# A weight product in plain float32 instead of three split products, and five converted layer-1 units ahead instead of two

## The chip, the cores and the metric

The kernel runs on one core of one Trainium2 chip. The metric is device time in microseconds (us) of one execution. Five engines work side by side, each through its own instructions in order: PE (TensorE, matrix products; its weight loads are listed as PEld), DVE (VectorE), ACT (ScalarE), POOL (GpSimd) and SP (SyncE, which here only issues transfers).

## The reference

Attention with normalised queries and keys, then two feed-forward blocks, in float32:

```python
q_n, k_n = rmsnorm(q, g_q), rmsnorm(k, g_k)        # 4 x 12 heads, 448 x 64
attn = softmax(q_n @ k_n.T / 8); x = attn @ v       # x: 1792 x 768
a = x @ w1; b = x @ w2                              # 768 x 1024 each
h = a * b @ w3                                      # 1024 x 1024
x = h @ w_out                                       # 1024 x 768
h = x @ w_in                                        # 768 x 2048
out = (h * clip(h + 3, 0, 6) / 6) @ w_out2          # 2048 x 768
```

The weights arrive as float64, the rest as float32.

## The kernel before

The 48 heads are taken as 24 pairs. Attention of a pair is eight steps; in step s PE makes two score products (L566, L567), DVE scales them and takes the row maximum (L573, L580), ACT the exponential (L585); eight steps later PE transposes (L592, four 112x112 pieces), ACT and DVE split the result into a high and a low part (L601, L611), and PE multiplies by v (L644, L645; for the first two pairs, which stay in plain float32, L640 and L626).

Around the attention steps `fill` feeds PE with other products. First comes `wprime`: (a*b) @ w3 @ w_out is computed as (a*b) @ (w3 @ w_out), and `wprime` makes w3 @ w_out once, as 128 products of a 128x128 piece of w3 with a 128x384 piece of w_out. It is written to memory in `evac` (ACT L223, DVE L224). Then follow `layer1` and `layer2` for the four batches of 448 tokens (L340, L345, and `mm3`, L81 to L83). When attention is over, PE goes on with layers 1 and 2 and then with the second feed-forward block.

Most products are made from split operands: a float32 value is kept as two rounded parts (float32r tiles), and `mm3` adds three products of parts. A weight unit on its way to such a pair costs: a load of float64 into one of four `raw` buffers, `convert` to float32 (ACT L137, L138, then DVE L140, L143), a copy of the high part (ACT L203) and a subtraction for the low part (POOL L205). These items form the list `order` in `open_wprime`: 16 halves of w3 ("a", 512 columns), 16 halves of w_out ("c", 384 columns), and 4 halves of w1 and w2 ("l") that give the first two units of layer 1. The other 14 units of layer 1 are converted in `open_l1` (ACT L287, POOL L289) while layer 1 runs. `rate` says how many us of PE work and of conversion work `fill` adds per attention step. A scheduler then fixes the order of instructions on each engine at build time.

In this text an attention step's number is the count of score pairs (L566 with L567) that stand before it on PE, or of L573 on DVE.

Of the kernel before, what the change touches and what calls it, by code (L numbers as in the profile page):

```python
# [12 lines left out]
F32 = mybir.dt.float32  # L13
F32R = mybir.dt.float32r
I32 = mybir.dt.int32
# [11 lines left out]
P = 128  # L27
# [3 lines left out]
DM = H * D  # L31
KD = DM // P
F1 = 1024
M1 = F1 // P
F2 = 2048
M2 = F2 // P
NH = DM // 2
# [3 lines left out]
LG = 8  # L41
AHEAD = 3
K3 = 12
SHIFT = {'ssum': -1, 'vsplit': -2, 'load_v': 2, 'rsum1': -1, 'ksplit': 4, 'rms1': 0}


@with_exitstack
def fused_kernel(ctx: ExitStack, tc: tile.TileContext, nat, qT, kT, vin, gq, gk,
                 w12, w3t, wo, win, wo2, outT):
    nc = tc.nc  # L50
# [5 lines left out]
    w12d = dpool.tile([M1, 2, P, 2 * DM], F32, name="w12d")  # L56
# [23 lines left out]
    def mm3(ps, lh, ll, rh, rl, first, last):  # L80
        nc.tensor.matmul(ps, lh, rh, start=first, stop=False)  # L81
        nc.tensor.matmul(ps, lh, rl, start=False, stop=False)  # L82
        return nc.tensor.matmul(ps, ll, rh, start=False, stop=last)  # L83
# [4 lines left out]
    def dma(out, src):  # L88
        return nc.sync.dma_start(out, src)
# [67 lines left out]
    W = {}  # L157

    def open_wprime():
        W["head"] = tc.tile_pool(name="head", bufs=1, side="right")  # L160
        W["hp"] = W["head"].__enter__()
        W["cm"] = tc.tile_pool(name="wprime", bufs=1, side="right")
        pool = W["cm"].__enter__()
        woh, w3, raw = {}, {}, {}
        HF = F1 // 2
        halves = [(a, h) for a in range(2, M1) for h in range(2)]
        order = [("a", 0, 0), ("a", 1, 0)] + [("c", c, 0) for c in range(4)] + [("a", 0, 1), ("a", 1, 1)]
        order += [("c", c, 0) for c in range(4, M1)] + [("c", c, 1) for c in range(M1)]
        order += [("a", a, h) for a, h in halves]
        order += [("l", z, h) for z in (1, 0) for h in range(2)]  # L170
        W["first"] = {}
        place = {o: q for q, o in enumerate(order)}
        W.update(pool=pool, woh=woh, w3=w3, place=place, free=0)

        def load(q):
            if q < len(order):
                kind, n, z = order[q]
                if kind == "a":
                    src = w3t[n][:, z * HF : z * HF + HF]
                else:  # L180
                    src = (wo[n] if kind == "c" else w12[0, n])[:, z * NH : z * NH + NH]
                raw[q] = fetch(pool, src, src.shape[1], "raw", 4)

        def item(q):
            kind, n, z = order[q]
            r = raw.pop(q)
            w = r.shape[1]
            if kind == "c":
                t = pool.tile([P, 2, NH], F32R, tag="woh", bufs=2 * M1, name="woh")
                woh[n, z] = (t[:, 0, :], t[:, 1, :])  # L190
            elif kind == "l":
                if z == 0:
                    W["first"][n] = W["hp"].tile([P, 2, DM], F32R, tag="ws", bufs=2, name="ws")
                t = W["first"][n][:, :, z * NH : z * NH + NH]
            else:
                t = pool.tile([P, 2, HF], F32R, tag="w3", bufs=4, name="w3")
                w3[n, z] = (t[:, 0, :], t[:, 1, :])
            f = r
            if r.dtype != F32:
                wi = r[:, :, 0]  # L200
                yield from convert(wi, r)
                f = wi.bitcast(F32)
            nc.scalar.activation(t[:, 0, :], f, AF.Copy)  # L203
            yield w / 1200
            W["sub"] = nc.gpsimd.tensor_sub(t[:, 1, :], f, t[:, 0, :])  # L205
            if kind == "l" and z == 1:
                dma(w12d[0, n], W["first"][n].bitcast(F32).rearrange("p t c -> p (t c)"))
            load(q + 4)
            yield 0.0

        for q in range(4):
            load(q)
        prep[0] = Prep([partial(item, q) for q in range(len(order))],
                       lambda: place["c", M1 - 1, 1] + (W["free"] if W["free"] < len(halves) else 99))

    def wprime():
        pool, place = W["pool"], W["place"]

        def evac(a, n, ps):
            h = NH // P  # L220
            st = pool.tile([P, h, 2, P], F32R, tag="wst", bufs=2, name="wst")
            src = ps[:, :NH].rearrange("p (n c) -> p n c", c=P)
            nc.scalar.activation(st[:, :, 0, :], src, AF.Copy)  # L223
            nc.vector.tensor_sub(st[:, :, 1, :], src, st[:, :, 0, :])  # L224
            for i in range(h):
                j, c = divmod((n * h + i) * M1 + a, 6)
                dma(wpd[j, :, c], st[:, i].bitcast(F32).rearrange("p t c -> p (t c)"))

        def mul(a, n, c, ps):
            h, l = W["w3"][a, c // 4]  # L230
            cs = slice(c % 4 * P, c % 4 * P + P)
            wh, wl = W["woh"][c, n]
            mm3(ps[:, :NH], h[:, cs], l[:, cs], wh, wl, c == 0, c == M1 - 1)

        def ready(a, n, c):
            return prep[0].ready(place["a", a, c // 4]) and prep[0].ready(place["c", c, n])

        for group in [(0, 1)] + [(a,) for a in range(2, M1)]:
            for n in range(2):
                acc = [bank("f") for _ in group]  # L240
                for c in range(M1):
                    for a, ps in zip(group, acc):
                        while not ready(a, n, c):
                            yield None
                        mul(a, n, c, ps)
                        yield 3 * 0.163
                    if n == 1 and c % 4 == 3:
                        W["free"] += len(group)
                for a, ps in zip(group, acc):
                    later(evac, a, n, ps)  # L250
        yield None
        yield None
        W["cm"].__exit__(None, None, None)
        open_l1()

    L = {}
# [3 lines left out]
    def open_l1():  # L260
        L["cm"] = tc.tile_pool(name="l1", bufs=1, side="right", **RW)
        pool = L["cm"].__enter__()
        raw, ws = defaultdict(list), {}
        L.update(ws=ws, xhl={}, abh={}, cur=0, pool=pool)
        pieces = [(u, h) for u in range(2, 2 * M1) for h in range(2)]
        pieces.reverse()

        def load():
            if pieces:
                u, h = pieces.pop()  # L270
                raw[u].append(fetch(pool, w12[u // 2, 1 - u % 2][:, h * NH : h * NH + NH], NH, "raw", 4))

        def item(u):

            if u < 2:
                ws[u] = W["first"][1 - u]
                return
            r = u % NU
            t = (W["hp"] if u % 5 < 2 else pool).tile([P, 2, DM], F32R, tag="ws", bufs=2 if u % 5 < 2 else 3, name="ws")
            if u < 2 * M1:  # L280
                for h, f in enumerate(raw.pop(u)):
                    cs = slice(h * NH, h * NH + NH)
                    if f.dtype != F32:
                        w = f[:, :, 0]
                        yield from convert(w, f)
                        f = w.bitcast(F32)
                    nc.scalar.activation(t[:, 0, cs], f, AF.Copy)  # L287
                    yield 0.35
                    nc.gpsimd.tensor_sub(t[:, 1, cs], f, t[:, 0, cs])  # L289
                    load()  # L290
                    yield 0.0
                dma(w12d[r // 2, 1 - r % 2], t.bitcast(F32).rearrange("p t c -> p (t c)"))
            else:
                src = w12d[r // 2, 1 - r % 2] if r < 2 * M1 else wpd[r - 2 * M1].rearrange("p k c -> p (k c)")
                dma(t.bitcast(F32).rearrange("p t c -> p (t c)"), src)
                yield 0.0
            ws[u] = t

        for _ in range(4):
            load()  # L300
        prep[0] = Prep([partial(item, u) for u in range(B * NU)], lambda: L["cur"] + AHEAD)
        for _ in range(4):
            prep[0].step()

    def xsplit(i):
# [106 lines left out]
    def attention(ap, rate):  # L412
# [185 lines left out]
        def thi(i, kb):  # L598
            ps, hi, lo = T["X", i, kb]
            if kb != 3 or i < K3 or full(i):  # L600
                nc.scalar.activation(hi, ps, AF.Copy)  # L601
# [188 lines left out]

    def rate(t):
        if "pool" not in L:
            return 1.05, 2
        if L["cur"] < 8:
            return 2.5, 4
        return 1.6, 2
# [6 lines left out]
    order = [B - 1] + list(range(B - 1))  # L803
# [53 lines left out]
    step, q = 0, 0  # L857
# [35 lines left out]
    for b, t in enumerate(order):  # L893
        acc = None
        for m in range(M2):
# [18 lines left out]
            ps = bank("s", "h2")  # L914
# [14 lines left out]
            u = lp.tile([P, S], F32, tag="u", bufs=2, name="u")  # L929
# [61 lines left out]
```

## Time and profile before

| | us |
|---|---|
| median of 3 runs | 1224.61 |
| the runs | 1225.72, 1224.61, 1220.15 |
| span of the profiled execution | 1219.5 |
| PE, DVE, ACT, POOL busy | 1160.4, 756.6, 726.6, 464.9 |

The profiled execution is known by its span alone; the runs are 0.7 to 6.2 us longer than it. "Busy" of PE is counted from modelled ends of pipelined products, so that a busy PE may still have room; the distance from one product's start to the next is the better measure.

### The profile page before, as it was taken

The numbers are of one execution on the slowest core, as the hardware profiler recorded it, in microseconds if no ns is written. First come the engines' busy times: TensorE is split into PE (matmuls) and PEld (weight loads), VectorE is DVE, ScalarE is ACT, GpSimd is POOL, SyncE is SP. The second block draws the span as 40 slices with busy tenths as digits, with TensorE's granted clock in tenths as the row PEclk, the third lists the DMA queues.
The fourth block names the chain that finished last, engine by engine and source line by source line (L and its number), as shares of the span: only waits on it lengthen the run. The fifth ranks groups of instructions, "written<-read, shape, count | busy, mean of one in ns | idle before, by whom it ended". The sixth has DMA issues, their size and how long they took to land.

```text
span 1219.5 us, 16961 instructions
## 1 busy us (share of the span) xinstructions
PE 1160.4 (95%) x5868; PEld 1020.5 (84%) x5868; DVE 756.6 (62%) x1474; ACT 726.6 (60%) x1401; POOL 464.9 (38%) x316
## 2 busy tenths in 40 slices
PE   3699998899999999999999999999999999999998
PEld 2457887777788999899999998999999999999997
DVE  6977888899976787677633447884333433343332
ACT  6888788899866767666634436664433443344332
POOL 3534224645522213212020005555455445544452
PEclk9799998999999999999999999999999999999999
DMA  7668565788987677666459985430200020001001
GB/s 277 209 220 239 191 188 196 251 284 293 334 265 254 222 224 249 228 240 197 148 187 360 355 304 207 156 101 23 91 1 1 4 88 1 1 1 46 1 1 46
DMA packets 64694, 203.73 MB, mean 167 GB/s; under 512 B 8544, under 2 KB 25440, under 8 KB 64608
## 3 DMA queue, kind: packets, MB, share of 16 engines
q1 hardware_dynamic: 64608, 202.65, 49.4%
q8 instruction: 46, 0.75, 0.3%
q14 instruction: 40, 0.33, 0.1%
HBM read 173.93 MB, written 28.68 MB: 166 GB/s over the span
## 4 chain that ended last, share of the span: by engine, by line
PE 75%; DVE 7%; ACT 5%; DMA 5%; issue 4%; POOL 3%; SPq 0%; ACTq 0%; POOLq 0%; DVEq 0%
PE bank L340 10%; PE acc L81 7%; PE acc L83 7%; PE acc L82 6%; PE h L81 6%; PE h L82 6%; PE h L83 6%; PE bank L345 5%; PE bank L592 4%; PE bank L81 3%; PE bank L82 3%; PE bank L83 3%; DVE PP L573 2%; PE bank L566 2%; PE bank L567 2%
## 5 line engine op out<-in xcount | busy, mean ns | idle before, releaser
L852 POOL TENSOR_TENSOR wis<-wf,wis 128x768 fp32r<-128x768 f32 x63 | 120.0, 1904 | 220.0 <-ACT wis L851 219.9
L340 PE MATMUL bank<-xhl,ws 128*128 128x448 f32 x768 | 184.9, 372 | 2.5 <-ACT bs L316 2.4
L931 DVE SCALAR_TENSOR_TENSOR u<-u,h 128x448 f32<-128x448 f32 x64 | 39.5, 618 | 210.6 <-ACT u L930 210.6
L340 PEld LDWEIGHTS bank<-xhl,ws 128*128 128x128 f32 x768 | 145.1, 191 | 16.5 <-ACT bs L316 3.1
L852 POOL TENSOR_TENSOR wos<-wf,wos 128x768 fp32r<-128x768 f32 x64 | 121.4, 1896 | 91.0 <-ACT wos L851 91.0
L585 ACT ACTIVATE PP<-PP,mx 112x448 f32<-112x448 f32 x192 | 127.2, 664 | 45.0 <-DVE mx L580 36.4
L573 DVE CUSTOM_DVE_ANT_0 PP<-bank,rb,rq 112x448 f32<-112x448 f32 x192 | 129.0, 675 | 34.8 <-PE bank L567 23.9
L83 PE MATMUL acc<-g,wos 128*128 128x448 f32 x384 | 141.3, 368 | 0.0
L82 PE MATMUL acc<-g,wos 128*128 128x448 f32 x384 | 141.3, 368 | 0.0
L81 PE MATMUL acc<-g,wos 128*128 128x448 f32 x384 | 140.0, 368 | 0.0
L81 PE MATMUL h<-x2h,wis 128*128 128x448 f32 x378 | 139.2, 368 | 0.5 <-DVE u L931 0.4
L82 PE MATMUL h<-x2h,wis 128*128 128x448 f32 x378 | 138.9, 367 | 0.0
L83 PE MATMUL h<-x2h,wis 128*128 128x448 f32 x378 | 137.4, 364 | 1.3 <-POOL wis L852 1.3
L930 ACT ACTIVATE u<-h,half 128x448 f32<-128x448 f32 x64 | 40.7, 636 | 156.0 <-PE h L83 156.0
L935 DVE TENSOR_TENSOR g<-u,g 128x448 fp32r<-128x448 f32 x64 | 105.2, 1645 | 37.5 <-ACT g L934 37.5
L851 ACT ACTIVATE wos<-wf 128x768 fp32r<-128x768 f32 x64 | 54.2, 847 | 85.9 <-PE acc L83 85.7
L601 ACT ACTIVATE xh<-bank 128x448 fp32r<-128x448 f32 (+1 forms) x156 | 83.0, 539 | 32.6 <-PE bank L592 29.4
L566 PE MATMUL bank<-K,Q 128*112 128x448 f32 x192 | 76.7, 400 | 25.6 <-DVE mx L573 13.1
L611 DVE TENSOR_TENSOR xl<-bank,xh 128x448 fp32r<-128x448 f32 x142 | 87.3, 616 | 21.9 <-ACT xh L601 20.6
L592 PE MATMUL bank<-ident,PP 112*128 112x112 f32 x672 | 94.4, 264 | 6.0 <-DVE xl L611 5.2
L592 PEld LDWEIGHTS bank<-ident,PP 112*128 112x128 f32 x672 | 77.7, 142 | 26.8 <-issue 6.8
L345 PE MATMUL bank<-xhl,ws 128*128 128x448 f32 x384 | 95.4, 367 | 0.0
(134 smaller groups left out, 2604.5 us busy)
## 6 DMA issues: line engine op xcount, KB each, us to landing
ws<-w12d SPq DMA_DIRECT2D x48, 768.0 KB
ws<-wpd SPq DMA_DIRECT2D x32, 768.0 KB
raw<-in_w_dram SPq DMA_DIRECT2D x32, 384.0 KB
w12d<-ws SPq DMA_DIRECT2D x16, 768.0 KB
wr<-in_wo_dram SPq DMA_DIRECT2D x16, 768.0 KB
qr<-in_qT_dram SPq DMA_DIRECT2D x24, 448.0 KB
kr<-in_kT_dram SPq DMA_DIRECT2D x24, 448.0 KB
nat<-in_nat_dram SPq DMA_DIRECT2D x23, 448.0 KB
```

The costliest lines, as they stand in the source:

```text
L81: nc.tensor.matmul(ps, lh, rh, start=first, stop=False)
L82: nc.tensor.matmul(ps, lh, rl, start=False, stop=False)
L83: return nc.tensor.matmul(ps, ll, rh, start=False, stop=last)
L340: nc.tensor.matmul(ps[:, :S], w[:, 0, ks], x[:, y, :], start=k == 0 and y == 0, stop=False)
L345: nc.tensor.matmul(ps[:, :S], w[:, 1, ks], L["xhl"][i][:, 0, :], start=False, stop=k == KD - 1)
L566: nc.tensor.matmul(ps[:CP, :S], qs, k1[:, j, :], start=True, stop=False)
L573: anchors[8 * i + s].append(nc.vector.tensor_tensor_reduce(out=T["PP", i][:, c, sl], in0=ps[:CP, :S], in1=T["rb", i][:, sl], op0=ALU.mult, ...
L585: anchors[8 * i + s].append(nc.scalar.activation(v, v, AF.Exp, bias=T["m", i][:, 8 + s : 9 + s], accum_out=T["sum", i][:, s : s + 1]))
L592: nc.tensor.transpose(ps[:, c * CP : c * CP + CP], src[:, c, kb * P : kb * P + P], ident[:CP, :CP])
L611: nc.vector.tensor_sub(lo, ps, hi)
L852: nc.gpsimd.tensor_sub(t[:, 1, :], wf[q], t[:, 0, :])
L935: nc.vector.tensor_sub(g[:, 1, :], u, g[:, 0, :])]
```

## The change

`wprime` multiplies plain float32 operands, one matmul where `mm3` made three; the converted w3 and w_out are no longer split, so that ACT L203 and POOL L205 go for them and `convert` writes straight into the operand tile. Eight halves of w3 are held, not four. Ten "l" halves (five units of layer 1), placed one after each remaining half of w3, take the place of four at the end of the list. `rate` adds up to 3, not 2, us of conversion work per step, and 1.3, not 1.05, us of PE work, while a product now counts 0.73 us, not 0.489.

```diff
 K3 = 12
+NF = 5
+NA3 = 8
...
-        order += [("a", a, h) for a, h in halves]
-        order += [("l", z, h) for z in (1, 0) for h in range(2)]
+        ones = [("l", u, h) for u in range(NF) for h in range(2)]
+        for a, h in halves:
+            order += [("a", a, h)] + ones[:1]
+            del ones[:1]
+        order += ones
...
+            if kind != "l":
+                if kind == "c":
+                    t = woh[n, z] = pool.tile([P, NH], F32, tag="woh", bufs=2 * M1, name="woh")
+                else:
+                    t = w3[n, z] = pool.tile([P, HF], F32, tag="w3", bufs=NA3, name="w3")
+                if r.dtype == F32:
+                    nc.gpsimd.tensor_copy(t, r)
+                else:
+                    yield from convert(t.bitcast(I32), r)
+                load(q + 4)
+                return
...
         def mul(a, n, c, ps):
-            h, l = W["w3"][a, c // 4]
             cs = slice(c % 4 * P, c % 4 * P + P)
-            wh, wl = W["woh"][c, n]
-            mm3(ps[:, :NH], h[:, cs], l[:, cs], wh, wl, c == 0, c == M1 - 1)
+            nc.tensor.matmul(ps[:, :NH], W["w3"][a, c // 4][:, cs], W["woh"][c, n], start=c == 0, stop=c == M1 - 1)
...
-                        yield 3 * 0.163
+                        yield 0.73
...
-        pieces = [(u, h) for u in range(2, 2 * M1) for h in range(2)]
+        pieces = [(u, h) for u in range(NF, 2 * M1) for h in range(2)]
...
-            return 1.05, 2
+            return 1.3, 3
```

Three places show how the order moves. On PE, at attention step 54 of either kernel, the product stands between scores (`K,Q`) and transposes (`ident,PP`); `woh` and `w` are the pieces of w_out and w3. Before:

```order
L81 MATMUL bank<-woh,w_1538 128x384
L82 MATMUL bank<-woh,w_1538 128x384
L83 MATMUL bank<-woh,w_1538 128x384
L81 MATMUL bank<-woh,w_1538 128x384
L82 MATMUL bank<-woh,w_1538 128x384
L83 MATMUL bank<-woh,w_1538 128x384
L592 MATMUL bank<-ident,PP 128x112 x4
L644 MATMUL bank<-xh,vo 128x448
L645 MATMUL bank<-xl,vo 128x448
L566 MATMUL bank<-K,Q 112x448
L567 MATMUL bank<-K,Q 112x448
```

And with the change:

```order
L574 MATMUL bank<-K,Q 112x448
L575 MATMUL bank<-K,Q 112x448
L241 MATMUL bank<-woh,w_995 128x384 x2
L600 MATMUL bank<-ident,PP 128x112 x4
L653 MATMUL bank<-xl,vo 128x448
L652 MATMUL bank<-xh,vo 128x448
L574 MATMUL bank<-K,Q 112x448
L575 MATMUL bank<-K,Q 112x448
L241 MATMUL bank<-woh,w_995 128x384 x2
```

Three products have become one. From step 40 to step 76 there are 53 of these, where 159 stood before; 71 (213) stand from step 4 to step 40.

On DVE, ahead of attention step 16, the first of the third pair (the L573, L581 at the end), stand the copy `rks` (from which the scale factors of that pair are written out and read back) and conversions (`raw`). Before:

```order
L492 TENSOR_SCALAR rq<-rr 112x16
L140 SCALAR_TENSOR_TENSOR raw<-raw 128x384
L511 COPY rks<-bank 16x112
L143 SCALAR_TENSOR_TENSOR raw<-raw 128x384
L140 SCALAR_TENSOR_TENSOR raw<-raw 128x384
L143 SCALAR_TENSOR_TENSOR raw<-raw 128x384
L224 TENSOR_TENSOR wst<-bank,wst 128x3x128 x2
L140 SCALAR_TENSOR_TENSOR raw<-raw 128x384
L143 SCALAR_TENSOR_TENSOR raw<-raw 128x384
L140 SCALAR_TENSOR_TENSOR raw<-raw 128x384
L143 SCALAR_TENSOR_TENSOR raw<-raw 128x384
L573 ISA PP,mx<-bank,rb,rq 112x448
```

And with the change, the last twelve rows ahead of the same step:

```order
L142 SCALAR_TENSOR_TENSOR raw<-raw 128x512
L145 SCALAR_TENSOR_TENSOR w_517<-raw 128x512
L142 SCALAR_TENSOR_TENSOR raw<-raw 128x384
L234 TENSOR_TENSOR wst<-bank,wst 128x3x128
L145 SCALAR_TENSOR_TENSOR raw<-raw 128x384
L234 TENSOR_TENSOR wst<-bank,wst 128x3x128
L142 SCALAR_TENSOR_TENSOR raw<-raw 128x512
L145 SCALAR_TENSOR_TENSOR w_569<-raw 128x512
L142 SCALAR_TENSOR_TENSOR raw<-raw 128x384
L145 SCALAR_TENSOR_TENSOR raw<-raw 128x384
L142 SCALAR_TENSOR_TENSOR raw<-raw 128x512
L145 SCALAR_TENSOR_TENSOR w_629<-raw 128x512
```

In all, 17 of the list's items stand ahead of step 16 before, and 27 with the change; 28 and 42 ahead of step 40.

On DVE at step 52 of the change no conversion (`raw`) stands between the attention's instructions; all 42 items of the list have been converted by step 40, and the next conversion stands at step 80:

```order
L581 ISA PP,mx<-bank,rb,rq 112x448
L581 ISA mx 112x1
L588 TENSOR_SCALAR mx<-mx 112x1
L234 TENSOR_TENSOR wst<-bank,wst 128x3x128
L581 ISA PP,mx<-bank,rb,rq 112x448
L581 ISA mx 112x1
L668 TENSOR_TENSOR xs<-bank,xs 64x448
L588 TENSOR_SCALAR mx<-mx 112x1
L619 TENSOR_TENSOR xl<-bank,xh 128x448
```

Before, 18 items stand between steps 40 and 76, as these do at step 71:

```order
L573 ISA PP,mx<-bank,rb,rq 112x448
L573 ISA mx 112x1
L464 TENSOR_SCALAR ss<-ss 112x32
L140 SCALAR_TENSOR_TENSOR raw<-raw 128x384
L580 TENSOR_SCALAR mx<-mx 112x1
L573 ISA PP,mx<-bank,rb,rq 112x448
L573 ISA mx 112x1
L140 SCALAR_TENSOR_TENSOR raw<-raw 128x384
L143 SCALAR_TENSOR_TENSOR raw<-raw 128x384
```

## Rows read from the trace of the kernel before

**Rows 1.** The page: busy time by engine, and the granted TensorE clock in 40 slices.

```profile
PE 1160.4 (95%) x5868; PEld 1020.5 (84%) x5868; DVE 756.6 (62%) x1474; ACT 726.6 (60%) x1401; POOL 464.9 (38%) x316
...
PEclk9799998999999999999999999999999999999999
```

**Rows 2.** Busy time by stretch: PE, PEld, DVE, ACT, POOL, granted clock, DMA share, GB/s.

```profile
0.00:26.00 26.00, 6.92 (x20) 4.98 (x21) 16.60 (x32) 15.18 (x27) 8.56 (x12) 1.00 0.76 265
26.00:137.00 111.00, 94.13 (x447) 67.03 (x445) 94.36 (x219) 92.19 (x203) 48.69 (x39) 0.92 0.72 227
137.00:253.00 116.00, 104.77 (x540) 87.90 (x540) 100.91 (x251) 93.86 (x211) 49.12 (x42) 0.91 0.63 205
253.00:318.00 65.00, 59.16 (x305) 48.37 (x304) 62.43 (x146) 58.45 (x132) 34.51 (x27) 1.00 0.88 293
318.00:600.00 282.00, 281.29 (x1552) 252.03 (x1551) 208.60 (x555) 193.12 (x424) 72.92 (x63) 1.00 0.72 239
...
760.00:1200.00 440.00, 440.00 (x2142) 401.71 (x2141) 192.78 (x172) 195.82 (x289) 223.78 (x120) 1.00 0.11 36
```

**Rows 3.** The score product L566 alone in the same stretches: PE, PEld, clock, DMA.

```profile
0.00:26.00 26.00, 2.25 (x4) 1.01 (x4) 1.00 0.76 265
26.00:137.00 111.00, 16.40 (x37) 6.69 (x37) 0.92 0.72 227
137.00:253.00 116.00, 14.79 (x36) 6.56 (x36) 0.91 0.63 205
253.00:318.00 65.00, 7.77 (x20) 3.49 (x21) 1.00 0.88 293
```

**Rows 4.** Groups of PE from 0 to 318 us, larger ones (L81 and L83 as L82).

```profile
L82 PE MATMUL bank<-woh,w 128*128 128x384 f32 x128 | 45.6, 356 | 1.5 <-POOL woh L205 1.4
...
L592 PE MATMUL bank<-ident,PP 112*128 112x112 f32 x296 | 43.3, 270 | 5.9 <-DVE xl L611 5.2 <-ACT xh L601 0.3 <-DVE mx L580 0.3
L340 PE MATMUL bank<-xhl,ws 128*128 128x448 f32 x168 | 43.3, 390 | 2.5 <-ACT bs L316 2.4
...
L645 PE MATMUL bank<-xl,vo 128*128 128x448 f32 x50 | 22.4, 448 | 4.1 <-DVE xl L611 2.4 <-DVE mx L580 1.8
L644 PE MATMUL bank<-xh,vo 128*128 128x448 f32 x51 | 21.3, 418 | 1.3 <-ACT xh L601 0.9 <-DVE rss L517 0.2
L345 PE MATMUL bank<-xhl,ws 128*128 128x448 f32 x84 | 20.9, 368 | 0.0
L640 PE MATMUL bank<-xh,vo 128*64 128x448 f32 x24 | 11.6, 565 | 0.0
```

**Rows 5.** The chain that ended last: start, us, work; stretches without a wait.

```profile
66.24 0.90 PE bank L640 x2
...
527.18 0.77 PE bank L592 x8
...
651.80 2.43 PE bank L340 x12
```

**Rows 6.** Timeline of PE: start, us; 29 products of 384 columns apart.

```profile
103.66 0.33 PE L83 MATMUL bank<-woh,w 128*128 128x384 f32 x1
...
108.69 0.33 PE L82 MATMUL bank<-woh,w 128*128 128x384 f32 x1
```

**Rows 7.** Timeline of DVE, 50 to 71 us (the L143 of 8 items).

```profile
50.38 0.55 DVE L143 SCALAR_TENSOR_TENSOR raw<-raw 128x384 int32<-128x384 int32 x1
...
51.43 1.39 DVE L143 SCALAR_TENSOR_TENSOR raw<-raw 128x384 int32<-128x384 int32 x1
...
66.73 1.27 DVE L143 SCALAR_TENSOR_TENSOR raw<-raw 128x384 int32<-128x384 int32 x1
70.61 0.68 DVE L573 CUSTOM_DVE_ANT_0 PP<-bank,rb,rq 112x448 f32<-112x448 f32 x1 [2.61 <-DMA raw<-in_wo_dram]
```

**Rows 8.** Timeline of POOL beside them.

```profile
50.38 3.44 POOL L547 TENSOR_TENSOR K<-kr,K 128x448 fp32r<-128x448 f32 x2
```

**Rows 9.** Groups of DVE by shape from 26 to 137 us.

```profile
L143 DVE SCALAR_TENSOR_TENSOR raw<-raw 128x384 int32<-128x384 int32 x14 | 11.7, 837 | 0.2
```

More of the change, by code (lines that the diff above doesn't have):

```diff
@@ L168, in open_wprime @@
         order += [("c", c, 0) for c in range(4, M1)] + [("c", c, 1) for c in range(M1)]
-        order += [("a", a, h) for a, h in halves]
-        order += [("l", z, h) for z in (1, 0) for h in range(2)]
+        ones = [("l", u, h) for u in range(NF) for h in range(2)]
[3 more added lines that the diff above has]
+        order += ones
         W["first"] = {}
         place = {o: q for q, o in enumerate(order)}
+        count = np.cumsum([o[0] == "a" for o in order] + [0])
         W.update(pool=pool, woh=woh, w3=w3, place=place, free=0)
@@ L180, in load @@
                 else:
-                    src = (wo[n] if kind == "c" else w12[0, n])[:, z * NH : z * NH + NH]
+                    src = (wo[n] if kind == "c" else w12[n // 2, 1 - n % 2])[:, z * NH : z * NH + NH]
                 raw[q] = fetch(pool, src, src.shape[1], "raw", 4)
@@ L187, in item @@
             w = r.shape[1]
[L188 to L197, printed above, removed]
+            if kind != "l":
[9 more added lines that the diff above has]
+                return
+            if z == 0:
+                W["first"][n] = W["hp"].tile([P, 2, DM], F32R, tag="ws", bufs=NF, name="ws")
+            t = W["first"][n][:, :, z * NH : z * NH + NH]
             f = r
@@ L205, in item @@
             W["sub"] = nc.gpsimd.tensor_sub(t[:, 1, :], f, t[:, 0, :])
-            if kind == "l" and z == 1:
-                dma(w12d[0, n], W["first"][n].bitcast(F32).rearrange("p t c -> p (t c)"))
+            if z == 1:
+                dma(w12d[n // 2, 1 - n % 2], W["first"][n].bitcast(F32).rearrange("p t c -> p (t c)"))
             load(q + 4)
@@ L213, in open_wprime @@
         prep[0] = Prep([partial(item, q) for q in range(len(order))],
-                       lambda: place["c", M1 - 1, 1] + (W["free"] if W["free"] < len(halves) else 99))
+                       lambda: int(np.searchsorted(count, NA3 + W["free"], "right")) - 1)
     def wprime():
@@ L273, in item @@
         def item(u):
-            if u < 2:
-                ws[u] = W["first"][1 - u]
+            if u < NF:
+                ws[u] = W["first"][u]
                 return
             r = u % NU
-            t = (W["hp"] if u % 5 < 2 else pool).tile([P, 2, DM], F32R, tag="ws", bufs=2 if u % 5 < 2 else 3, name="ws")
+            t = W["hp"].tile([P, 2, DM], F32R, tag="ws", bufs=NF, name="ws")
             if u < 2 * M1:
@@ L301, in open_l1 @@
         prep[0] = Prep([partial(item, u) for u in range(B * NU)], lambda: L["cur"] + AHEAD)
-        for _ in range(4):
+        for _ in range(2 + NF):
             prep[0].step()
```

## The prediction

> **What bounds the kernel now.** I read the page's busy times first, then stretches, then PE's groups and distances, then the places where DVE and POOL wait. PE is busy 95% of the span [rows 1], but this is not spread evenly: from 318 us to the end PE is busy without a break but for a few us, while from 26 to 318 us it is busy 85 to 91% [rows 2]. Even that is too much, since starts tell more than modelled ends. A 384-column product of `wprime` takes (108.69 - 103.66)/29 = 0.173 us [rows 6]; a 448-column one 2.43/12 = 0.203, a transpose piece 0.77/8 = 0.096, a plain float32 product of 448 columns (two records) 0.90 [rows 5]. Up to 318 us PE holds 384 products of `wprime`, 296 transpose pieces, 168 + 84 + 50 + 51 and about 2 x 96 products of 448 columns and 12 float32 products [rows 3, 4]: 66.6 + 28.4 + 110 + 10.8 = 216 us of work in 318. Nearly 100 us are room, some 26 of them at the start. So the end is set by the work on PE plus the idle time that is left in the first 318 us; whatever is added to PE there must be paid by idle time that goes.
>
> What holds PE up there is DVE first: 94 of 111 us busy, then 101 of 116, then 62.4 of 65 (96%), with ACT close behind at 83, 81 and 90% [rows 2]. The stretches are cut at attention steps 4, 40, 76 and 96, by the count of scores [rows 3]; I call them A (26 to 137), B (137 to 253) and C (253 to 318). In A and B the mean granted clock is 0.92 and 0.91 [rows 2], and no later slice dips [rows 1]: for a part of these stretches it was at the lower of its two levels, 1.2 GHz.
>
> **What the change adds: PE.** 384 products of 0.173 (66.6 us) go, 128 plain float32 ones come. The trace has such a product only with 64 columns of weights and 448 moving columns: 0.90 [rows 5]. By columns alone 384 would take 0.77. Below lies 4 x 0.173 = 0.69, if nothing but four plain passes is paid. Above: 448 columns at 2.4 GHz are 0.187, four times 0.75, which leaves 0.15 for the weight loads; twice that for 128 columns of weights, on 4 x 0.16, is 0.94. I take 0.83, between 0.77 and the row's own 0.90. In total 106 us, or 40 more than before (0.69: +22; 0.94: +54).
>
> The Trainium skill says on its page FP8 and Floating Point Precision, section TensorE Precision Notes, that true float32 takes four passes of the array. By that alone the sum would have +22; the row of 0.90, where four passes of 0.203 are 0.81, is dearer, and the sum goes by the row. It also speaks against a change that puts four passes where three were.
>
> **What it takes away: ACT, POOL, and DVE's waits.** 32 copies on ACT and 32 subtractions on POOL go. Six "l" items move forward from C, with all that they issue: a load for each half and a store for each unit, which SP had issued later. POOL's work is dear to DVE: an L143 that takes 0.55 us alone took 1.39 beside a subtraction of POOL [rows 7, 8], and the 14 such of A have a mean of 0.837 [rows 9], 4.0 us over 0.55 in this group alone. By the order, 24 of some 35 subtractions in A go and 8 of 384 columns come, so that I give DVE back about 6 us there over all its groups.
>
> This is what the Trainium skill's page SBUF — State Buffer, section Who interferes with whom, says of a DVE instruction with two SBUF inputs beside a GpSimd instruction that reads SBUF: the second to come waits for the whole of the first. The trace agrees (0.55 against 1.39), and by the rule the wait goes with each subtraction that goes.
>
> **Stretch by stretch.** The order of the change gives the counts.
>
> A (steps 4 to 40). DVE gets 73 conversion passes where 46 were: 27 x 0.55 = +15, less the 6, so 94 + 9 = 103 us busy; at 85% as now this is 121 us, at 90% 115. PE has 71 x 0.83 + 92 x 0.203 + 98 x 0.096 + 12 x 0.90 = 98. I take 118, 7 more than before. The wait to watch is ahead of step 16: ten more items stand there in DVE's order, and all attention is queued behind them. Before, seven items from 50.38 to 66.73 took 2.3 us each, and step 16 then began after 2.61 us of waiting for one more transfer [rows 7]: transfers and the hand from ACT to DVE to ACT to POOL set this pace, since a `raw` buffer came free only after POOL. Now it comes free after DVE, so I expect 1.6 us or less.
>
> B (steps 40 to 76). No conversion is left: DVE loses 37 passes, 37 x 0.55 = 20 of 101 us, and ACT the two steps and the copy of the same 18 items. PE has 53 x 0.83 + (72 + 74) x 0.203 + 128 x 0.096 = 86 us and becomes the bound. At 95% (later stretches reach nearly all) that is 90 us, 26 less than the 116 of before. That PE waits less should keep the clock at 2.4 GHz, where B had 0.91 [rows 2]; this is in the 95%.
>
> C (steps 76 to 96). Layer 1's products pushed out of B come here: 245 where 164 were. PE has (245 + 80) x 0.203 + 72 x 0.096 = 73 us, and DVE, at 96% now, gets 44 passes for 35. At 95% of PE this is 77 us, 12 more.
>
> After step 96 both orders hold the same work (247 and 252 products of layer 1 are done by then), and PE has no room [rows 2]. What layer 1 still loads is 11 units, not 14, which costs nothing: transfers and ACT lie under PE, which is busy 281 of 282 us there.
>
> The sum is +7 - 26 + 12 = -7 us on a span of 1219.5. The median of the runs is 5.1 above that span, which I take to stay: 1224.6 - 7 = 1217.6. A difference under 0.5% (6 us) can't be told from no change here.
>
> **Rivals.** First, the float32 product costs no more than four passes, 0.69. B then has 79 us of PE work, and DVE with about 78 is beside it: 84 us, 32 less; A gains 2. -32 + 5 + 12 = -15, 1209 to 1210. The rule of four passes above gives this; 0.90 against 0.81 in the row speaks against it.
>
> Second, slower: the ten items ahead of step 16 keep their 2.3 us. That is 23 us more there; the way from step 16 to 40 gets no shorter for it (15 items stand there, 11 before). With 2 us of it covered by DVE's relief, A is +21: 21 - 26 + 12 = +7, 1231 to 1232. It decides from about 2.0 us per item. For it: the 2.61 us of waiting for a transfer [rows 7]. Against it: A's transfers ran at 227 GB/s, and 293 were had in C [rows 2].
>
> Third, no difference: the product costs 0.94. B's PE work is 92, at 95% 97, so -19, and A gets 9 to 10: 9 - 19 + 12 = +2, 1226 to 1227. For it: all weights have 128 columns here.
>
> **How the numbers follow.** I give the forecast 0.42, cheap products 0.22, the slow step 16 0.18, the dear product 0.18. The forecast itself spans -13 to 0 (A between 115 and 121, the rest of B and C a few us), about 0.6 of it beyond 6 us. Faster: 0.42 x 0.6 + 0.21 + 0.03 = 0.49. Slower: 0.17 + 0.04 = 0.21. Same: 0.30. The range reaches from a little below the cheap product with A at 115 (1203) to the slow step 16 with a pace slightly above (1234); the forecast's own range is 1211 to 1225.
>
> **What would show it.** The distance between the new products' starts gives 0.83 or another number. L573 of step 16 starts at about 75 us (70.6 before; over 90 would be the second rival). Step 40's score stands at about 144 us, step 76 at 234, step 96 at 311. Between steps 40 and 76 PE should have next to no gaps and a clock near 1.00. L143's mean should fall from 0.84 to about 0.65. I would be wrong if PE still waits in B for ACT or DVE, whose sequence of steps has a latency that busy shares don't show, or if C, with its units of layer 1 due at once, holds PE up longer than the 12 us.

## The result, and the profile after

| | before | after |
|---|---|---|
| median of runs beside one another, us | 1223.13 (4 runs) | 1206.63 (4 runs) |
| ratio, 95% interval | | 0.9872 [0.9845, 0.9898] |
| span of the profiled execution, us | 1219.5 | 1203.6 |

The change takes 1.3% off, 16 us; the forecast was 7 us. The whole range, 1203 to 1234, holds the time, the forecast's own, 1211 to 1225, does not. The page of after, where [rows 1] stood before:

```profile
PE 1161.3 (96%) x5740; PEld 998.9 (83%) x5740; DVE 739.1 (61%) x1474; ACT 711.5 (59%) x1369; POOL 427.8 (36%) x284
...
PEclk9799999999999999999999999999999999999999
```

After the first three slices the page shows no dip. In windows of 10 us one is left in A, 0.85 from 120 to 130 us; from 140 us on all have 1.00, where before has lower ones up to 260. The busy times by stretch, cut at the same attention steps (4, 40, 76, 96) as in [rows 2], which now stand at 26, 142, 226 and 304 us:

```profile
0.00:26.00 26.00, 9.27 (x21) 5.11 (x21) 14.54 (x32) 14.00 (x25) 3.07 (x8) 1.00 0.74 269
26.00:142.00 116.00, 100.87 (x370) 58.53 (x369) 98.85 (x248) 96.53 (x211) 32.37 (x25) 0.91 0.88 290
142.00:226.00 84.00, 80.67 (x387) 56.05 (x387) 71.03 (x202) 66.55 (x152) 25.57 (x22) 1.00 0.57 170
226.00:304.00 78.00, 75.41 (x405) 66.10 (x404) 71.40 (x169) 66.40 (x150) 39.07 (x32) 1.00 0.75 247
304.00:600.00 296.00, 295.97 (x1636) 265.66 (x1635) 221.97 (x574) 203.36 (x444) 76.31 (x64) 1.00 0.72 236
```

A is 5 us longer, B 32 shorter at a clock of 1.00 (0.91 before), C 13 longer. A's clock is 0.91, much as before (0.92). PE's busy time is the same as before to 1 us, which shows how little it tells: with each product counted at its own distance from the next, PE has more work and far less idle time. The products, in the timeline of PE:

```profile
189.95 1.45 PE L241 MATMUL bank<-woh,w 128*128 128x384 f32 x4
...
104.52 0.97 PE L648 MATMUL bank<-xh,vo 128*64 128x448 f32 x2
105.42 0.60 PE L600 MATMUL bank<-ident,PP 112*128 112x112 f32 x4
```

A plain float32 product is two records. Four records take 1.45 us, and one of them lasts 0.48 (the median of the line), so that they start (1.45 - 0.48)/3 = 0.32 apart and a product takes 0.643 us by the exact starts. That is 4 x 384 columns at 2.4 GHz (0.640), with nothing left for the weight load, whereas the one with 64 columns of weights is still 105.42 - 104.52 = 0.90. The 128 products take 82.3 us for 66.6 before: the change puts 16 us on PE, not 40.

What stands against that is idle time: the span of a stretch less its products at full-clock distances (0.643, 0.173, 0.203, 0.095 for a transpose piece, 0.90), so that time lost to the lower clock counts as idle.

| PE idle, us | to step 4 | A | B | C | to 700 us in all |
|---|---|---|---|---|---|
| before | 22.5 | 32.6 | 27.3 | 10.6 | 99.8 |
| after | 21.1 | 29.8 | 8.3 | 4.7 | 69.7 |

Some 30 us less of idle time and 16 more of work leave -14 by 700 us, a further -1 to -2 comes later, and the spans differ by 15.9. B alone gives 19 of the 30.

The wait that I had named, step 16 of DVE (L573, now L581), and the work ahead of it, from DVE's timeline:

```profile
64.99 0.56 DVE L142 SCALAR_TENSOR_TENSOR raw<-raw 128x384 int32<-128x384 int32 x1 [2.86 <-ACT raw L140]
...
79.99 0.56 DVE L142 SCALAR_TENSOR_TENSOR raw<-raw 128x384 int32<-128x384 int32 x1 [2.03 <-ACT raw L140]
...
82.90 0.68 DVE L581 CUSTOM_DVE_ANT_0 PP<-bank,rb,rq 112x448 f32<-112x448 f32 x1
```

and what ACT waited for from 46 to 83 us (total, times, longest):

```profile
ACT raw L139 <- DMA raw<-in_wo_dram: 5.2, 3, 3.0
ACT raw L139 <- DMA raw<-in_w3t_dram: 4.4, 3, 2.7
ACT raw L139 <- DMA raw<-in_w_dram: 1.1, 1, 1.1
```

Step 16 starts at 82.9, 12.3 us later than before [rows 7], and DVE waited 9.9 us on the way for ACT, which itself waited 10.7 for transfers. Ten more items cost 1.2 us each, and ACT's waits for transfers are the larger part of it. Yet step 40 is only 4.8 us later. And DVE's L143, now L145, from 26 to 142 us, the shapes of 384 columns, for the mean of 837 ns in [rows 9]:

```profile
L145 DVE SCALAR_TENSOR_TENSOR woh<-raw 128x384 int32<-128x384 int32 x14 | 8.8, 632 | 0.1
L145 DVE SCALAR_TENSOR_TENSOR raw<-raw 128x384 int32<-128x384 int32 x10 | 5.9, 589 | 0.1
```

### The profile page after: what moved, and what is told of

It is laid out like the page before. It is cut to its first block, busy times and chain, and to the rows that moved or that the text cites. A ratio compares the mean times of both kernels' runs of the same rounds, so it can differ in the third digit from the quotient of the medians.

```text
span 1203.6 us, 16598 instructions
## 1 busy us (share of the span) xinstructions
PE 1161.3 (96%) x5740; PEld 998.9 (83%) x5740; DVE 739.1 (61%) x1474; ACT 711.5 (59%) x1369; POOL 427.8 (36%) x284
## 4 chain that ended last, share of the span: by engine, by line
PE 84%; issue 4%; DVE 4%; ACT 3%; DMA 3%; POOL 1%; SPq 0%; ACTq 0%; DVEq 0%; POOLq 0%
PE bank L348 13%; PE acc L85 7%; PE acc L84 7%; PE acc L83 7%; PE h L83 6%; PE h L84 6%; PE h L85 6%; PE bank L353 6%; PE bank L600 5%; PE bank L241 3%; PE bank L574 3%; PE bank L575 2%; PE bank L84 2%; PE bank L83 2%; PE bank L85 2%
## 5 line engine op out<-in xcount | busy, mean ns | idle before, releaser
L348 PE MATMUL bank<-xhl,ws 128*128 128x448 f32 x768 | 179.9, 367 | 0.0
L593 ACT ACTIVATE PP<-PP,mx 112x448 f32<-112x448 f32 x192 | 127.7, 667 | 48.9 <-DVE mx L588 46.4
L581 DVE CUSTOM_DVE_ANT_0 PP<-bank,rb,rq 112x448 f32<-112x448 f32 x192 | 129.1, 676 | 28.4 <-PE bank L575 22.9
L83 PE MATMUL acc<-g,wos 128*128 128x448 f32 x384 | 140.0, 368 | 0.0
L83 PE MATMUL h<-x2h,wis 128*128 128x448 f32 x378 | 139.0, 368 | 0.0
L943 DVE TENSOR_TENSOR g<-u,g 128x448 fp32r<-128x448 f32 x64 | 102.6, 1602 | 38.7 <-ACT g L942 38.7
L241 PE MATMUL bank<-woh,w 128*128 128x384 f32 x256 | 102.1, 526 | 8.6 <-DVE wst L234 4.9
L574 PE MATMUL bank<-K,Q 128*112 128x448 f32 x192 | 81.7, 427 | 19.6 <-ACT K L553 10.9
L609 ACT ACTIVATE xh<-bank 128x448 fp32r<-128x448 f32 (+1 forms) x156 | 82.9, 541 | 29.7 <-PE bank L600 26.8
L600 PEld LDWEIGHTS bank<-ident,PP 112*128 112x128 f32 x672 | 78.6, 141 | 26.2 <-issue 10.9
L619 DVE TENSOR_TENSOR xl<-bank,xh 128x448 fp32r<-128x448 f32 x142 | 87.0, 617 | 12.9 <-ACT xh L609 11.6
```

The costliest lines, as they stand in the source:

```text
L241: nc.tensor.matmul(ps[:, :NH], W["w3"][a, c // 4][:, cs], W["woh"][c, n], start=c == 0, stop=c == M1 - 1)
L348: nc.tensor.matmul(ps[:, :S], w[:, 0, ks], x[:, y, :], start=k == 0 and y == 0, stop=False)
L574: nc.tensor.matmul(ps[:CP, :S], qs, k1[:, j, :], start=True, stop=False)
L581: anchors[8 * i + s].append(nc.vector.tensor_tensor_reduce(out=T["PP", i][:, c, sl], in0=ps[:CP, :S], in1=T["rb", i][:, sl], op0=ALU.mult, ...
L593: anchors[8 * i + s].append(nc.scalar.activation(v, v, AF.Exp, bias=T["m", i][:, 8 + s : 9 + s], accum_out=T["sum", i][:, s : s + 1]))
L600: nc.tensor.transpose(ps[:, c * CP : c * CP + CP], src[:, c, kb * P : kb * P + P], ident[:CP, :CP])
```

## Experiments

The theory behind all of them: the end is PE's work plus its idle time in the first 320 us, and the change wins because conversions are done ahead of step 40, so that from then on PE has something that it can do more of the time. The rivals are that one part alone brings the gain: the relief of ACT and POOL, the rates, or the units that are ready early. Each time is a median beside runs of before on the same chip (1222.3 to 1223.4); after was timed on one of these chips alone. "Idle" is counted as above: the column 100 is from 100 to 200 us of the span.

| kernel | us | ratio [95%] | idle 0 | 100 | 200 | 300 | to 700 | span |
|---|---|---|---|---|---|---|---|---|
| before | | 1 | 51.3 | 19.1 | 16.7 | 8.4 | 99.8 | 1219.5 |
| after | 1206.6 | 0.9872 [0.9845, 0.9898] | 45.1 | 8.4 | 10.4 | 2.8 | 69.7 | 1203.6 |
| product alone | 1220.7 | 0.9976 [0.9957, 0.9994] | 40.9 | 7.6 | 22.4 | 7.0 | 82.7 | 1218.1 |
| conversion rate alone | 1224.7 | 1.0014 [0.9998, 1.003] | 50.1 | 16.7 | 23.8 | 9.9 | 105.7 | 1225.4 |
| after, two units | 1227.3 | 1.0026 [1.0007, 1.0046] | 45.5 | 3.8 | 26.2 | 10.2 | 89.0 | 1224.2 |
| after, four units | 1209.2 | 0.9894 [0.9859, 0.9928] | 45.5 | 5.5 | 12.8 | 4.8 | 72.4 | 1206.5 |
| after, rates 1.05, 2 | 1240.8 | 1.0145 [1.0113, 1.0177] | 46.0 | 24.5 | 16.9 | 14.0 | 104.2 | 1238.1 |
| after, rates 1.05, 3 | 1238.5 | 1.0125 [1.0099, 1.0152] | 45.8 | 17.9 | 16.7 | 19.0 | 102.2 | 1236.3 |
| after, rates 1.3, 2 | 1225.2 | 1.003 [1.0013, 1.0047] | 40.4 | 19.9 | 14.1 | 12.0 | 89.4 | 1223.5 |
| after, rates 1.5, 3 | 1218.2 | 0.9968 [0.9951, 0.9986] | 46.5 | 10.7 | 14.5 | 6.8 | 83.1 | 1218.9 |
| after, slow until step 16 | 1220.5 | 0.9981 [0.9963, 0.9998] | 40.9 | 22.3 | 11.0 | 6.2 | 83.9 | 1217.8 |
| after, POOL's work back | 1212.6 | 0.9923 [0.9895, 0.995] | 46.4 | 10.5 | 12.1 | 4.6 | 76.8 | 1211.6 |
| after, ACT's work back | 1218.0 | 0.9969 [0.995, 0.9989] | 48.6 | 14.3 | 12.1 | 2.9 | 81.1 | 1214.9 |

In every row with the plain product the span is that of before, plus 16, less the idle time saved, to within 2 us. That has to be so, since idle is what PE's work leaves of the span; it says only that little changes behind 700 us. What the rows show is how much idle time each part takes away, and where.

**The product alone, and the conversion rate alone**, each in the kernel before.

```diff
...
-            mm3(ps[:, :NH], h[:, cs], l[:, cs], wh, wl, c == 0, c == M1 - 1)
+            nc.tensor.matmul(ps[:, :NH], W["w3"][a, c // 4][:, cs], W["woh"][c, n], start=c == 0, stop=c == M1 - 1)
```

```diff
-            return 1.05, 2
+            return 1.05, 3
```

> The plain float32 product alone on the kernel before: same list of items (two units ahead), same rates. Own theory (the end is PE work plus idle time of PE in the first 318 us; the product adds 16 us of work, and the copies and subtractions that go give back idle time): about -6 us against before, span 1213 to 1216, with 0.643 us per product and more PE idle in steps 40 to 96 than the change has. Rival (the five units ahead carry the gain): no gain or a loss up to the 16 us, span 1220 to 1235.

> The kernel before with 3, not 2, us of conversion work per step and nothing else. Rival (the rates alone carry the gain): about -10 to -16 us. Own theory: conversions are only moved earlier, none goes, ACT and POOL stay as loaded as before: within 4 us of before.

Measured: -2.7 us and +1.3 us, both under 0.3%; my -6 was too much, the second line held. The product alone saves 17 us of idle time, which pays for its 16 us of work and no more: it clears the stretch from 100 to 200 us, and the idle time then shows up from 200 to 300 (22.4, more than before), where two units of layer 1 are ready and the third is not. PE's longest waits from 200 to 300 us are for such units (L286, the copy of a converted unit) and for attention:

```profile
PE bank L339 <- ACT ws L286: 3.9, 4, 1.7
PE bank L565 <- DVE mx L572: 3.5, 5, 1.1
```

Neither part carries the gain. The product alone was not quite alone: `fill` still counted 0.489 us for what takes 0.643, so that 1.05 us per step was in truth 1.05 x 0.643/0.489 = 1.38, and layer 1 began at step 65 (68 before).

**Fewer units ahead.** The rest of the change stays; with two, the ring of buffers is also that of before.

```diff
-NF = 5
+NF = 2
...
```

> The change with two units ahead instead of five; product and rates as changed. Own theory: six halves (6 x 1.1 us on DVE, 6 x 1.5 on ACT) go back to where layer 1 runs and DVE was at 96%; about 6 us of the 16 are lost, span 1208 to 1212. Rival (the units ahead carry the gain): 12 us or more lost, span 1216 or more. Rival (they are idle decoration): span 1202 to 1205.

> The changed kernel with four units of layer 1 converted ahead instead of five (the ring of units one smaller too). Two units took 20.7 us more than five. If each unit ahead is worth the same, 7 us of it per unit: 1211 to 1216 us. If the last one is not needed, since layer 1's later units are then converted in time: 1205 to 1209 us.

Measured: two units 20.7 us above after, four 2.5 us. With two, the rival that gives the units the gain came true and my line did not; with four, the second reading. The edit for four leaves the ring of buffers at five, although its text has it one smaller. With two, PE's waits from 220 to 400 us, the first three and the fifth of that view:

```profile
PE bank L574 <- DVE mx L581: 4.4, 3, 2.3
PE bank L640 <- DVE mx L581: 3.8, 1, 3.8
PE bank L653 <- DVE mx L588: 2.3, 1, 2.3
...
PE bank L353 <- POOL ws L297: 1.5, 2, 1.1
```

and its windows from 226 us on (clock third from the end):

```profile
226.00:304.00 78.00, 68.23 (x332) 56.09 (x331) 67.43 (x159) 62.60 (x141) 34.61 (x29) 0.93 0.72 238
304.00:400.00 96.00, 91.63 (x485) 78.56 (x484) 73.83 (x179) 70.71 (x156) 38.19 (x32) 0.98 0.85 284
```

Up to 220 us this kernel is the better one by 3 us of idle time; then its attention waits for DVE, which converts the missing units between the steps, and the clock is at its lower level for a part of the stretch, where after has 1.00. The third and the fourth unit are worth 18 us together; the fifth cannot be told from nothing, since the two intervals overlap.

**The rates.** `rate` of the changed kernel returns other numbers.

```diff
-            return 1.3, 3
+            return 1.05, 2
```

> The change with the old rates (1.05 us of PE work and 2 of conversion work per step). Layer 1 then begins at attention step 90, not 76. Own theory: PE gets less beside attention and waits more, 5 to 10 us lost, span 1209 to 1214. Rival (the rates carry the gain): all 16 lost, span 1219. Rival (rates are indifferent): span 1202 to 1206.

> The change with 1.3 us of PE work but 2, not 3, us of conversion work per step. Both old rates together lost 34 us. If the PE rate carried that, this is within 4 us of the change; if the conversion rate did, 20 us or more are lost; own theory expects the PE rate (layer 1 begins late, PE waits beside attention), so 3 to 10 us lost here.

> The changed kernel with 1.05 us of PE work per step instead of 1.3, conversions still at 3. By the order layer 1 begins at step 90, not 76; 40 items stand ahead of step 40 (42). My theory (the end is the work of PE plus its idle time in the first part): between steps 40 and 90 PE is given too little to do, idles some 10 us more and shows a granted clock below 1.00 in slices where 1.3 had 1.00; 1217 to 1224 us. Rival (only the rate of conversions matters, since all of the loss with both old rates is gone when it is 3 again): 1205 to 1210 us.

> The changed kernel with 1.5 us of PE work per step instead of 1.3. By the order layer 1 begins at step 66, not 76; 85 products stand ahead of step 40 (74). If PE's idle time in the first 320 us is still to be had by more work in hand, up to 5 us less, 1201 to 1206 us. Rival (the units of layer 1 aren't converted in time, DVE and ACT are the bound from step 66): PE waits for them, 1208 to 1216 us.

Measured: against after, 1.05 with 2 costs 34.1 us, 1.05 with 3 31.8, 1.3 with 2 18.6, 1.5 with 3 11.6. My line for both old rates (5 to 10 us lost) and both of my lines on 1.05 with 3 missed: the rate of PE work is worth most, far more than the 10 to 17 us that I had given it. My 3 to 10 us for 1.3 with 2 were too few as well. The trace says why for 1.05. From step 40 to 64 before has 52 products of `wprime` (of three parts, 0.520 together) in 24 steps, 52 x 0.520/24 = 1.13 us of work per step; after has 43, 43 x 0.643/24 = 1.15; with 1.05 it is 34, or 0.91. Since a product now counts 0.73 in `fill` and not 0.489, 1.05 feeds PE less per step than before, and 1.3 is what it was. The 31.8 us are thus the price of feeding PE less, not a gain that 1.3 brings over before. With 1.05 the last product of `wprime` stands at 245 us (after: 214), attention steps come sooner for it (step 76 at 223, not 226), and PE waits between them, and later for layer 1, as in its waits from 240 to 400 us:

```profile
PE bank L640 <- ACT xh L609: 3.5, 1, 3.5
PE bank L348 <- ACT ws L295: 3.5, 2, 2.3
PE bank L574 <- DVE mx L581: 3.4, 5, 1.3
```

With 1.3 and 2, 12 conversion passes stand on DVE between 142 and 226 us (after: 1), and PE's waits from 100 to 200 us for ACT's high part and DVE's row maximum are 5.1 and 4.1 us (after: 1.9 and none).

More than 1.3 is no better: with 1.5 step 40 is at 153 us (142), layer 1 begins at step 66, attention ends 29 us later, and idle time comes back, most of it from 200 us on. That is just past the 1208 to 1216 us of the rival. My hope of a kernel that beats both fell.

**A slow start.** Conversions at 2 until step 16, then at 3. I took the 12 us by which step 16 is late for a cost that could be had back.

```diff
-            return 1.3, 3
+            return (1.3, 2) if t < 16 else (1.3, 3)
```

> The change with 2 us of conversion work per step until attention step 16, then 3 as changed: 22, not 27, items stand ahead of step 17 on DVE. Own theory (the attention queues behind those items, 12 us late at step 16): step 16 starts some 6 us sooner, but most of the delay was made good by step 40 anyway: 0 to 4 us gained. Rival (the delay ahead of step 16 is free): no difference in time and in step 40.

Measured: 13.8 us slower than after, where I had hoped for up to 4 less. Step 16 does come sooner, at 76.9 us, but step 40 comes later, at 145.3. From 120 to 160 us, this kernel and then after:

```profile
120.00:160.00 40.00, 30.03 (x113) 19.77 (x114) 34.44 (x77) 27.93 (x62) 15.96 (x12) 0.79 0.72 240
```

```profile
120.00:160.00 40.00, 37.38 (x169) 25.44 (x169) 36.11 (x97) 32.84 (x74) 12.86 (x10) 0.96 0.70 233
```

PE does 113 instructions instead of 169, at a clock of 0.79, and in this stretch it waits 4.1 us for DVE's low part (L619) and 4.4 for ACT's high part (L609), where after waits 0.6 and 1.9. The five items that were not done ahead of step 16 now stand between attention steps. So the late step 16 is no loss. DVE and ACT have time to spare ahead of it, 20.6 and 21.5 us busy of 31, and little behind it, as two windows of after show:

```profile
52.00:83.00 31.00, 24.98 (x85) 13.06 (x84) 20.64 (x41) 21.54 (x48) 5.46 (x5) 0.89 0.88 287
83.00:142.00 59.00, 56.70 (x237) 35.04 (x237) 52.59 (x139) 52.63 (x117) 21.13 (x17) 0.97 0.91 299
```

**POOL's and ACT's work put back.** Each converted piece of w3 and w_out gets one more instruction, a subtraction on POOL or a copy on ACT, 32 in all, whose result nobody reads; the output is unchanged.

```diff
+                d = pool.tile([P, HF], F32, tag="dump", bufs=2, name="dump")
+                nc.gpsimd.tensor_sub(d[:, :w], t, t)
```

```diff
+                d = pool.tile([P, HF], F32, tag="dump", bufs=2, name="dump")
+                nc.scalar.activation(d[:, :w], t, AF.Copy)
```

> The change with 32 subtractions put back on POOL, each reading the converted piece of w3 or w_out twice and writing to a tile that nobody reads (so the output is the same). They stand in steps 0 to 40, where DVE converts. Own theory: DVE gets back the waits that went, some 6 us in that stretch, half of which shows in the end: 2 to 6 us lost, and the mean of the second conversion pass on DVE rises. Rival (POOL's release of DVE carries the gain): 10 us or more lost. Rival (it does not matter): within 1 us.

> The change with 32 copies put back on ACT, each of a converted piece into a tile that nobody reads. ACT gets about 16 us more in steps 0 to 40. Own theory: ACT is at 80 to 90% there and the exponentials queue behind the copies: 3 to 7 us lost. Rival (ACT is off the path): within 1 us.

Measured: POOL's 32 cost 6.0 us, as expected, ACT's 11.4, more than expected. The first is the cleanest of all these experiments: by the traces PE, DVE and ACT do the same instructions in the same order as in after, and only POOL's 32 come in between. The two intervals just touch, but each of its four runs (1211.9 to 1213.3) is above each of after's (1205.4 to 1211.1). With POOL's work back, the second group of L145 from 26 to 142 us reads

```profile
L145 DVE SCALAR_TENSOR_TENSOR raw<-raw 128x384 int32<-128x384 int32 x10 | 7.8, 784 | 0.1
```

784 ns for 589. Over all of DVE's instructions up to 220 us, the time beyond what each form takes undisturbed (the mean of the shortest tenth of its records) is 33 us before, 18 after and 28 here. ACT's copies were the dearer, which I had not given a term of its own: ACT is the first of the hands in each conversion and makes attention's exponentials too. They don't slow DVE's instructions (15 us by the same count), but they also changed the order on PE and DVE, so that the 11.4 are not the copies' time alone.

**Why 0.90 and not 0.75.** The v pieces of the first two pairs get 128 columns, 64 of them zeros (POOL clears these once for each pair).

```diff
...
-                nc.tensor.matmul(T["pv", i, j][:64, :S], vo[:, j, kb % 4], hi, start=kb == 0, stop=kb == 6)
+                nc.tensor.matmul(T["pv", i, j][:, :S], vo[:, j, kb % 4].rearrange("p a d -> p (a d)"), hi,
+                                 start=kb == 0, stop=kb == 6)
```

> One look at the price of a plain float32 product. The v pieces of the first two pairs get 128 columns instead of 64, the added 64 columns being zeros; the rest is the changed kernel. First reading (64 columns of weights are what leaves part of the weight load exposed): the two records of such a product of 448 columns stand 0.373 us apart, 0.747 for the product, four times 448 columns at 2.4 GHz, as the products of 384 columns do with 0.643. Second reading (something else at that place, the transposes or the score products beside them, makes it dear): it stays at 0.427 and 0.470, 0.90 for the product. The span is expected within 0.3% of the changed kernel's by both.

Measured, in one run:

```profile
109.49 0.92 PE L650 MATMUL bank<-xh,vo 128*128 128x448 f32 x2
110.24 0.55 PE L601 MATMUL bank<-ident,PP 112*128 112x112 f32 x4
```

110.24 - 109.49 = 0.75: the first reading holds. Where score products follow, the two records and the first score product behind them take 0.97 us, for 1.20 in after. The 0.15 us that I had taken for weight loads belong to narrow weights alone. The kernel gains nothing by it (span 1208.0, 4.4 above after, or 0.4%, with 12 x 0.15 = 1.8 us less work): by the trace the edit changed the order of instructions on PE, DVE and ACT, and the idle time moved by several us with it. A difference of that size between kernels of different order, as that of four units, says nothing of a cause.

## Why the prediction was right

**The mechanism held, the forecast's size did not**: 16 us for 7, outside its own 1211 to 1225. PE's work plus idle time sets the end; conversions leave B, PE becomes its bound (76 us of work in 84, DVE busy 71), the clock stays at 1.00 there. The stretches were forecast at +7, -26 and +12 and came at +5.4, -31.7 and +12.9, with another 2 us after step 96, where I had none. These are nearly the numbers of the first rival, +5, -32 and +12, to which I had given 0.22. The median, which I took to stay 5.1 us above the profiled span, stands 3.0 above it. Steps 40, 76 and 96 were to stand at 144, 234 and 311 us and stand at 141.7, 226.4 and 304.2. L143's mean was to fall to about 0.65 and fell to 0.632 and 0.589.

**The mis-sized term is the price of the product**: 0.83 taken, 0.643 measured, below the lower bound of 0.69. The step that failed put the 0.90 of 64-column weights down to 448 columns plus a load that 128 columns would not shorten. The Trainium skill's rule (FP8 and Floating Point Precision, TensorE Precision Notes: four passes for true float32) agrees with 0.643, where four passes of 384 columns at 2.4 GHz are 0.640; the first rival went by it, at 0.69. My lower bound erred too: the split product's 0.173 is 0.013 above 384 columns at 2.4 GHz, and the plain product doesn't pay that four times.

**A second error hid the first.** With 0.643 my own working would have given B 76/0.95 = 80 us, 36 less, and A, bounded by DVE at 90% of 103, 115 us, 4 more: -36 + 4 + 12 = -20, 1205 by the median, below the time that came. B's share of work came at 90%, not 95: 8 us are still lost there, and PE's waits for DVE and ACT, which I had said could stay, are 3.2 us of them by the trace; the rest has no name in it. So "next to no gaps" was wrong. That the first rival has B's 84 us is in part luck: it took PE's product too dear (0.69) and DVE's 78 us beside it, which came as 71.

**The second rival was half there.** Step 16 was late by 12.3 us, not 4 (75 forecast, with no sum beside it, 82.9 measured), held in large part by transfers, as it said; it still left only 4.8 us at step 40. That the way from step 16 to 40 "gets no shorter" was the rival's wrong step, and the slow start shows that the early conversions are no loss. The 2.61 us of [rows 7], which spoke for it, I had not looked into: L573 reads `rb`, not `raw`, and `rb`'s transfer (issued at 62.20) signals on the same semaphore as the later `raw` that the profile names, so that it waited, as far as the trace tells, for the scale factors read back.

**DVE's relief** was 6 us in A by my estimate; by the count of the experiments it was 9.5, and POOL's work put back takes all of it and costs 6.0 us in the end. This agrees with the Trainium skill's rule on the page SBUF — State Buffer, section Who interferes with whom: 589 against 784 ns as POOL's subtractions come back. The copies of ACT, for which the sum had no number, cost 11.4 when put back, a change of order included.

**That the parts can be costed one by one** is what the working took for granted, and it does not hold. Product and conversion rate, taken alone, give -2.7 and +1.3 us; the units, the PE rate and the conversion rate, taken out one by one, cost 20.7, 31.8 and 18.6, each more than the whole gain of 16.5. PE idles wherever the first of its suppliers is late, and a part that mends one place only moves the idle time to the next.

Open stays how the loss with a rate of 1.05 divides between PE's waits for attention, for layer 1's units and the lower clock, which occur together. Two parts were never taken out or put in by themselves: the eight halves of w3 that are held, not four, and 1.3 us of PE work in the kernel before. How much of the 16 us is the order that the scheduler happened to make is not known either.

## What to carry to other kernels

Where one engine sets the end with work plus waits, sum the waits by stretch and ask of a change where the next supplier is late; a dearer product is paid for if it empties the stretch in which PE waited. Do preparatory work while its engines have time to spare, even if that makes a visible step later. When the cost of one item changes in a planner's books, its budget per step changes with it: check how much real work a step still gets.

## What the runs showed that I had not expected

A plain float32 product with 128 columns of weights takes no more than four passes of its columns (0.643 us for 384 columns, 0.75 for 448), one with 64 columns 0.15 us more (0.90). That these 0.15 us are its weight load is not shown. The Trainium skill's page TensorE: Matmul & The Clock Gate, section Weight-path perf modes, gives a faster weight load for 128 columns, but not for FP32; here there is a step between 64 and 128 columns in float32 too, and no run shows whether it has the same cause.

Two of the slower kernels show a lower granted clock in the stretches where PE waits more: 0.79 from 120 to 160 us in the slow start and 0.93 from 226 to 304 us with two units, where after has 0.96 and 1.00. A part of what such a wait costs is therefore that products behind it run at 1.2 GHz. It does not fall at each wait: from 220 to 240 us PE of after idles 5 of 20 us, and the clock stays at 1.00.
